# The first loads of a 2:4-pruned matmul: one weight load, two loads of x moved, four fillers fewer

## The chip, the core and the metric

The kernel runs on one core of a Trainium2 chip. The core has five engines that matter here: TensorE (PE in the profile; its weight loads are PEld), VectorE (DVE), ScalarE (ACT), GpSimd (POOL) and SyncE (SP). SyncE and ScalarE issue DMAs, each on a queue of its own. The metric is the device time of one execution in microseconds (us); the time before is the median of three runs.

## What is computed

```python
B, S, D = 16, 512, 1024              # x: [16, 512, 1024], w: [1024, 1024], b: [1024], all bf16
G = D // 4
wg = w.reshape(G, 4, D)
mag = jnp.abs(wg)
order = jnp.argsort(mag, 1)
thr = jnp.take_along_axis(mag, order[:, 2:3, :], 1)   # second largest of each four
wp = (wg * (mag >= thr)).reshape(D, D)                # 2:4 pruning along the rows
return jnp.einsum("bsd,df->bsf", x, wp) + b
```

In each column of w, of every four neighbouring rows those stay whose magnitude reaches the second largest of the four; the rest become zero. Then x times the pruned w, plus a bias.

## The kernel before, in words

The 8192 rows of x are 64 tiles of 128 rows. The weights are held as two halves of the rows (g = 0 and 1), each as four interleaved row classes (m = 0 to 3), so that the four members of a pruning group lie in one partition. The first half is pruned in four pieces of 256 columns (pieces 0 to 3), the second half in two of 512 (pieces 4 and 5).

Before pruned weights exist, TensorE cannot do useful work. So the kernel starts in this way:

- **Loads** (lines 118 to 129). `load_w` (L100) loads a piece of the weights, some of its row classes only if it is told so; `load_x` (L103) loads the first 512 columns of some tiles of x. Both go through `issue` (L96), so every DMA of theirs is recorded at L98. SyncE loads classes 0 and 1 of piece 0, then tiles 3-4, tile 2, piece 1, tiles 0-1, and further weights. ScalarE loads classes 2 and 3 of piece 0, then tiles 5-6, and after that runs a dummy activation on one element (L121), which brings in ScalarE's function table.
- **Fillers** (L136, called at L404 and L405). TensorE multiplies constants into a PSUM bank that nobody reads: six matmuls of 512 columns and then 14 short ones of 128 columns. They stand in TensorE's queue ahead of all real work.
- **An order written out by hand** (`order`, L266). For each engine a list of tokens. T3a is the transpose of tile 3 on TensorE (four instructions at L193), C3a the copy of its result by ScalarE (L198), M3.0yp a group of matmuls of tile 3 with piece 0 (L229; the letters name row classes and column halves), and abs0a, hi0a, lo0, ..., mult0yp, ... are VectorE's steps of the pruning of piece 0 (L169 for abs, L159 for the rest). TensorE's list begins T3a T4a T5a T6a T2a M3.0yp M4.0yp. VectorE's list begins abs0a abs0b, where abs0a reads classes 0 and 1 of piece 0 and abs0b classes 2 and 3. The token mult2t is the step of piece 2 whose product M3.2t reads.
- **Matmuls with whole rows** (`nat`, L240). The pruned weights are written back in row order by DMAs (`spread`, L144), and tiles 7 to 63 are multiplied with x transposed by DMA. `close` (L451) ends the tiles that were begun early; the loop at L472 does the batches of 4 and 8 tiles. VectorE adds the bias (L437 or L439), ScalarE issues the stores; for the last LATE tiles (L46) each half of the columns is stored by itself (L492).

Every DMA raises one of eight semaphores, which are used in rotation; before a semaphore is used again, the issuing queue waits for the earlier DMA on it.

## Time and profile before

| | |
|---|---|
| median of 3 runs | 232.76 us (232.62 to 232.9) |
| the profiled execution, its own time | 232.89 us |
| span in the profile, first to last instruction | 231.1 us |
| TensorE busy | 226.6 us of the span |
| VectorE busy | 107.9 us |
| ScalarE busy | 14.0 us |

In the rows of the timeline the first number is the start in us from the span's start, the second the time from the first start to the last end in the row, xN the number of instructions merged into it, and in brackets stands the idle time of the engine ahead of it and what ended that. PEld is the loading of the stationary operand, which precedes each matmul. In rows of a DMA view the last number is the time from issue to landing. In rows of the chain the second number is that instruction's share of the chain.

### The profile page before, as it was taken

The numbers are of one execution on the slowest core, as the hardware profiler recorded it, in microseconds if no ns is written. First come the engines' busy times: TensorE is split into PE (matmuls) and PEld (weight loads), VectorE is DVE, ScalarE is ACT, GpSimd is POOL, SyncE is SP. The second block draws the span as 40 slices with busy tenths as digits, with TensorE's granted clock in tenths as the row PEclk, the third lists the DMA queues.
The fourth block names the chain that finished last, engine by engine and source line by source line (L and its number), as shares of the span: only waits on it lengthen the run. The fifth ranks groups of instructions, "written<-read, shape, count | busy, mean of one in ns | idle before, by whom it ended". The sixth has DMA issues, their size and how long they took to land.

```text
span 231.1 us, 2851 instructions
## 1 busy us (share of the span) xinstructions
PE 226.6 (98%) x1142; PEld 110.9 (48%) x1162; DVE 107.9 (47%) x200; ACT 14.0 (6%) x27; POOL 17.6 (8%) x15
## 2 busy tenths in 40 slices
PE   8999999999999999999999999999999999999995
PEld 5986444444444444444444444444444444444443
DVE  3999877844424424424424424423423423433434
ACT  2874100000000000000000000000000000000000
POOL 1000199700000000000000000000000000000000
PEclk9999999999999999999999999999999999999999
DMA  6999999997399422991259821693128932122122
GB/s 203 276 197 280 164 217 223 297 320 252 124 206 232 155 91 72 237 281 64 75 116 252 222 94 71 162 298 134 65 91 198 273 122 83 54 91 91 53 86 91
DMA packets 79308, 38.19 MB, mean 165 GB/s; under 512 B 64192, under 2 KB 71744, under 8 KB 79296
## 3 DMA queue, kind: packets, MB, share of 16 engines
q1 hardware_dynamic: 68384, 20.75, 43.6%
q10 hardware_dynamic: 10912, 17.27, 20.9%
q8 instruction: 9, 0.15, 0.3%
q14 instruction: 3, 0.02, 0.0%
HBM read 3.28 MB, written 16.78 MB: 87 GB/s over the span
## 4 chain that ended last, share of the span: by engine, by line
PE 98%; issue 0%; DVE 0%
PE ps L242 88%; PE ps L229 5%; PE tp L242 2%; PE ps L138 2%; PE tp L193 1%; PE ps L193 0%; DVE o L437 0%
## 5 line engine op out<-in xcount | busy, mean ns | idle before, releaser
L242 PE MATMUL ps<-wp_nat,xb 128*128 128x512 bf16 (+1 forms) x831 | 178.9, 375 | 0.9
L242 PEld LDWEIGHTS <-xb 128*128 128x128 bf16 x848 | 82.2, 98 | 97.7
L437 DVE TENSOR_TENSOR o<-ps,bias_sb 128x512 bf16<-128x512 f32 (+1 forms) x112 | 71.6, 677 | 113.7 <-PE ps L242 111.4
L433 POOL TENSOR_TENSOR st<-st,bias_sb 128x1024 f32<-128x1024 f32 x8 | 16.7, 2142 | 0.0
L242 PE MATMUL ps<-wp_nat,xlead 128*128 128x512 bf16 x63 | 14.7, 379 | 0.1
L242 PEld LDWEIGHTS <-xlead 128*128 128x128 bf16 x88 | 8.6, 98 | 10.2
L229 PE MATMUL ps<-wp,xt 128*128 128x256 bf16 (+1 forms) x130 | 12.8, 258 | 0.0
L439 DVE TENSOR_TENSOR o<-ps,st 128x512 bf16<-128x512 f32 x16 | 11.1, 691 | 2.8 <-PE ps L242 2.2
L229 PEld LDWEIGHTS <-xt 128*128 128x128 bf16 x130 | 10.9, 98 | 1.1
L242 PE MATMUL ps<-wp_nat,xlow 128*128 128x512 bf16 x47 | 10.6, 379 | 0.1
L264 ACT COPY st<-ps 128x512 f32<-128x512 f32 x14 | 7.4, 600 | 3.2 <-PE ps L229 3.1
L242 PEld LDWEIGHTS <-xlow 128*128 128x128 bf16 x48 | 4.7, 98 | 5.7
L159 DVE TENSOR_TENSOR mag<-mag,hi 128x256 bf16<-128x256 bf16 (+2 forms) x15 | 6.1, 435 | 0.1
L159 DVE TENSOR_TENSOR wp<-w_sb,mag 128x256 bf16<-128x256 bf16 (+2 forms) x15 | 6.1, 435 | 0.1
L242 PE MATMUL tp<-wp_nat,xlead 128*128 128x512 bf16 x23 | 5.8, 380 | 0.0
L138 PE MATMUL ps<-const-bfloat16-1.0 128*128 128x128 bf16 (+1 forms) x20 | 4.2, 408 | 0.8 <-PEq L510 0.8
L169 DVE TENSOR_SCALAR mag<-w_sb 128x512 uint16<-128x512 uint16 (+2 forms) x5 | 2.3, 473 | 3.5 <-DMA w_sb<-in_w_dram 3.5
L138 PEld LDWEIGHTS <-const-bfloat16-1.0 128*128 128x128 bf16 x20 | 2.3, 146 | 2.4 <-issue 2.4
L159 DVE TENSOR_TENSOR hi<-mag 128x512 bf16<-128x512 bf16 (+2 forms) x7 | 3.2, 458 | 0.1
L159 DVE TENSOR_TENSOR lo<-mag 128x512 bf16<-128x512 bf16 (+1 forms) x6 | 3.1, 509 | 0.0
L193 PEld LDWEIGHTS <-x 128*128 128x128 bf16 x28 | 2.3, 124 | 0.3 <-DMA x<-in_x_dram 0.2
L422 POOL COPY pruned<-wp 128x1 bf16<-128x1 bf16 x1 | 0.2, 187 | 26.7 <-DVE wp L159 26.7
(18 smaller groups left out, 18.8 us busy)
## 6 DMA issues: line engine op xcount, KB each, us to landing
out_dram<-o ACTq DMA_DIRECT2D x58, 256.0 KB, 2.4
wp_nat<-wp SPq DMA_DIRECT2D x14, 128.0 KB, 3.2
out_dram<-o ACTq DMA_DIRECT2D x10, 128.0 KB, 1.7
w_sb<-in_w_dram SPq DMA_DIRECT2D x2, 512.0 KB, 5.5
w_sb<-in_w_dram SPq DMA_DIRECT2D x3, 256.0 KB, 5.1
x<-in_x_dram SPq DMA_DIRECT2D x2, 256.0 KB, 4.3
x<-in_x_dram ACTq DMA_DIRECT2D x1, 256.0 KB, 4.0
bias_sb<-in_b_dram SPq DMA_DIRECT2D x1, 256.0 KB, 4.7
```

The source lines that it names most:

```text
L138: pe(nc.tensor.matmul(warm_ps[:, :rep * P], lhsT=nc.const_aps.tensor(1.0, [P, P], bf16), rhs=nc.const_aps.tensor(1.0, [P, rep * P], bf16), ...
L159: dve(nc.vector.tensor_tensor(out, a, b_, op=op))
L169: dve(nc.vector.tensor_single_scalar(mag.bitcast(u16), w_.bitcast(u16), 0x7FFF, op=Alu.bitwise_and))
L193: pe(nc.tensor.transpose(tp[:, m, :], xg[:, m, :], ident[:]))
L229: pe(nc.tensor.matmul(ps[:, c0 + d:c1 + d], lhsT=xpk[t][:, m, :], rhs=wp[:, g, m, c0:c1], start=(new and m == ms.start), stop=(left[key] = ...
L242: pe(nc.tensor.matmul(ps, lhsT=xt[:, kt - koff, :], rhs=wp_nat[:, kt, c0:c1], start=(kt == first), stop=(kt == last)))
L264: act(nc.scalar.copy(staged[(q, h)][:, at, :, :].rearrange("p t c -> p (t c)"), ps_open.pop(key)[:]))
L422: pool(nc.gpsimd.tensor_copy(out=pruned[:], in_=wp[:, 1, 3, Dout - 1:]))
L433: pool(nc.gpsimd.tensor_tensor(st[:], st[:], bias.to_broadcast([P, 2, 2, CW]), op=Alu.add))
L437: dve(nc.vector.tensor_tensor(o[:, c0:c1], ps, bias_sb[:, c0:c1], op=Alu.add))
L439: dve(nc.vector.tensor_tensor(o[:, c0:c1].rearrange("p (n c) -> p n c", n=2), ps.rearrange("p (n c) -> p n c", n=2), add, op=Alu.add))
```

## The change

The first 256 columns of the weights are loaded by one DMA on SyncE's queue instead of by two on two queues. The load of tiles 3-4 follows directly behind it. ScalarE's load of tiles 5-6 now stands behind the dummy activation in ScalarE's program. There are ten short fillers instead of 14. LATE goes from 6 to 7, so one more tile is stored in two halves. VectorE's abs0a and abs0b stay two instructions; both now read what the one load brings.

```diff
-    LATE = 6
+    LATE = 7
...
-    load_w(0, 0, 256, 0, 2)
-    load_w(0, 0, 256, 2, 4, "act")
+    load_w(0, 0, 256)
+    load_x(3, 5)
+    act(nc.scalar.activation(spark[:], nc.const_aps.tensor(1.0, [P, 1], bf16), Act.Abs))
     load_x(5, 7, "act")
-    act(nc.scalar.activation(spark[:], nc.const_aps.tensor(1.0, [P, 1], bf16), Act.Abs))
-    load_x(3, 5)
     load_x(2, 3)
...
     filler(6, 4)
-    filler(14)
+    filler(10)
```

## The prediction

> **What bounds the kernel now.** I read the page first (busy shares, then the chain that ended last), then the chain in order of time, then the waits of the first 40 us. The page:

> ```profile
> span 231.1 us, 2851 instructions
> ...
> PE 226.6 (98%) x1142; PEld 110.9 (48%) x1162; DVE 107.9 (47%) x200; ACT 14.0 (6%) x27; POOL 17.6 (8%) x15
> ...
> PE 98%; issue 0%; DVE 0%
> ```

> TensorE (PE) is the chain from beginning to end. The change neither adds nor removes a matmul of the result, so it can act in one way only: by moving the moment at which TensorE goes from fillers to real work, or by making TensorE stop later. The chain's head and one later piece:

> ```profile
> 0.77 4.21 PE ps L138 x20
> 4.99 1.02 PE tp L193 x8
> 6.01 0.51 PE ps L193 x8
> 6.52 0.22 PE tp L193 x4
> ...
> 42.17 10.74 PE ps L242 x49
> ```

> Twenty fillers (L138), then 20 transposes (L193) of tiles 3, 4, 5, 6, 2, then matmuls. The waits of the first 40 us, two of them:

> ```profile
> DVE mag L169 <- DMA w_sb<-in_w_dram: 3.5, 1, 3.5
> ...
> PEld L193 <- DMA x<-in_x_dram: 0.2, 1, 0.2
> ```

> So two loads set the start: VectorE's pruning waits 3.5 us for the first weights, TensorE 0.24 us for tiles 3-4. After that TensorE never waits. The weight loads and matmuls at the switch:

> ```profile
> 3.29 1.43 PEld L138 LDWEIGHTS <-const-bfloat16-1.0 128*128 128x128 bf16 x13 [0.28 <-issue]
> 4.96 1.04 PE L193 MATMUL tp<-ident,x 128*128 128x128 bf16 x8
> 5.80 0.72 PE L193 MATMUL ps<-ident,x 128*128 128x128 bf16 x8
> 6.35 0.39 PE L193 MATMUL tp<-ident,x 128*128 128x128 bf16 x4
> ```

> Here the reader sees the **clock**: eight transposes from 4.96 to 5.80 are 0.105 us each; the last four in the chain take 0.22, so 0.055 each; the eight between need 0.55, which is two slow and six fast. TensorE thus runs at half speed up to 5.80 + 0.21 = 6.01 us and at full speed from there.

> **The change part by part.**

> *Ten short fillers.* A short filler is (1.43 - 0.15) / 12 = 0.107 us. The weight loads of the fillers end at 4.72; with four fewer they end at 4.72 - 0.43 = 4.29. Worth nothing by itself: TensorE already waits behind them. It decides only if tiles 3-4 land before 4.72; otherwise the pause grows.

> *LATE 7.* One 256 KB store of the seventh tile from the end becomes two of half the size. By the chain's 10.74 us for 49 matmuls, a matmul is 0.22 us, and 6 tiles of 16 matmuls are 21 us: the stores lie that far from the end. Cost 0. There is one load less and one store more, so the eight DMA semaphores are in the same rotation at the end.

> *The loads.* The issues of before, and their times to landing (DMA view at each issue's window):

> ```profile
> 0.73 0.45 SPq L98 DMA_DIRECT2D w_sb<-in_w_dram  x1
> 1.24 0.96 SPq L98 DMA_DIRECT2D x<-in_x_dram  x2
> 2.25 0.68 SPq L98 DMA_DIRECT2D w_sb<-in_w_dram  x1
> 0.74 0.50 ACTq L98 DMA_DIRECT2D w_sb<-in_w_dram  x1
> 1.26 0.49 ACTq L98 DMA_DIRECT2D x<-in_x_dram  x1
> 1.79 1.28 ACT L121 ACT_TABLE_LOAD   x1 [1.79 <-issue]
> 3.08 0.20 ACT L121 ACTIVATE spark<-const-bfloat16-1.0 128x1 bf16<-128x1 bf16 x1
> ```

> ```profile
> w_sb<-in_w_dram ACTq DMA_DIRECT2D x1, 128.0 KB, 2.9
> x<-in_x_dram SPq DMA_DIRECT2D x1, 256.0 KB, 3.7
> x<-in_x_dram ACTq DMA_DIRECT2D x1, 256.0 KB, 4.0
> w_sb<-in_w_dram SPq DMA_DIRECT2D x1, 256.0 KB, 4.5
> x<-in_x_dram SPq DMA_DIRECT2D x1, 256.0 KB, 5.0
> ```

> Before: the second half of the weights lands at 0.74 + 2.9 = 3.64, tiles 3-4 at 1.24 + 3.7 = 4.94, tiles 5-6 at 1.26 + 4.0 = 5.26. And the DMA engines, from 2.6 to 4.3 us:

> ```profile
> 2.60:4.30 1.70, 1.70 (x13) 1.17 (x11) 0.80 (x4) 0.68 (x2) 0.00 (x0) 1.00 1.00 334
> ```

> The last two columns are the share of the DMA engines and GB/s: they are full, at 334. (The column before them, the clock, says 1.00 there, which the spacing of the matmuls contradicts; I go by the spacing.) So what counts is the order in which bytes are asked for. The three loads together (768 KB) are done at 5.26 in whatever order they go, and a load moved behind another frees its 256 KB / 334 GB/s = 0.78 us.

> *When does ScalarE issue tiles 5-6?* This decides the case. No row of before shows a DMA issued behind a running activation. The bounds are 0.8 us (ScalarE's sequencer hands over the table load and the Abs, neither of which waits for anything, and goes on) and 0.74 + 1.28 + 0.20 = 2.2 us (it stays until both are done). The nearest rows:

> ```profile
> 20.36 0.59 ACT L264 COPY st<-tp 128x512 f32<-128x512 f32 x1
> L98 ACTq EVENT_SEMAPHORE  x71: 17/17/17, 20.4 to 228.4; - x71
> 28.14 16.74 POOL L433 TENSOR_TENSOR st<-st,bias_sb 128x1024 f32<-128x1024 f32 x8
> L521 POOLq DRAIN  x3: 34/78/16641, 28.3 to 230.8; - x3
> ```

> ScalarE's first semaphore instruction runs at 20.4, while the copy begun at 20.36 still has 0.5 us to go. GpSimd's sequencer stands at its closing drain at 28.3, with eight adds of 16.74 us in total handed over. Sequencers run ahead of their engines here, so I take **0.8 us**: tiles 5-6 are then asked for 0.46 us earlier than before, not later.

> [...]

> *Weights.* One 256 KB load on one queue. Bounds for its landing: 3.5 us (where the first half lands now: VectorE starts at 3.50) and 0.73 + 4.5 = 5.2 (the next 256 KB of weights, which stand behind other loads). Nearest are the two halves, at 3.64; tiles 5-6, asked for earlier, take part of the engines, at most 0.78 us of it, and by how early they come about a third. I take 3.9, so VectorE starts s = 0.4 us later. Its first operation waited for half of the weights and now waits for all; behind it stands VectorE's whole pruning chain, and behind that the matmuls of L229.

> *What stands behind on SP's queue.* The first issue grows from 0.45 to at most 0.68 us (the row at 2.25, as many bytes), so tile 2, the next weights and tiles 0-1 are issued up to 0.23 later. With the engines full they land by bytes, and those ahead of them are the same; cost 0, unless tile 0 slips (its room is below).

> *Tiles 3-4.* Last of the three in this order, so between 4.94 and 5.26; I take 5.15, and TensorE starts at 5.19. Slow transposes until 6.01: 0.82 / 0.105 = 7.8. The other 12.2 at 0.055 take 0.67, to 6.68. The same sum for before: 1.05 / 0.105 = 10, 10 x 0.055 = 0.55, to 6.56. Loss **0.12 us**. The 0.23 us of later start is halved since it falls in the slow clock.

> *Does VectorE's 0.4 us come through?* These pairs are a product of VectorE (start, duration) and the weight load of TensorE's first matmul that reads it (the first and the 75th load of L229, by the order list M3.0yp and M3.2t); the last is the first transpose of tile 0, loaded at 2.96 + 5.0 = 7.96:

> ```profile
> 5.80 0.28 DVE L159 TENSOR_TENSOR wp<-w_sb,mag 128x256 bf16<-128x256 bf16 x1
> 6.52 0.15 PEld L229 LDWEIGHTS <-xt 128*128 128x128 bf16 x2
> 12.49 0.28 DVE L159 TENSOR_TENSOR wp<-w_sb,mag 128x256 bf16<-128x256 bf16 x1
> 13.07 0.10 PEld L229 LDWEIGHTS <-xt 128*128 128x128 bf16 x1
> 8.23 0.11 PEld L193 LDWEIGHTS <-x 128*128 128x128 bf16 x1
> ```

> Room is 0.44, 0.30 and 0.27 us. With VectorE 0.4 later and TensorE 0.12 later, M3.2t's room is 0.30 - 0.40 + 0.12 = 0.02: just enough. So the sum is +0.12. The profiled execution took 232.89 us, 231.1 of it span and 1.8 around it; it would become 233.01. The median of the runs is 232.76, 0.13 below it, so the forecast is 232.76 + 0.12 = **232.9 us**.

> **The rivals.**

> *B, the change does what it says:* ScalarE holds the issue to 2.2 us. Tiles 3-4 then stand behind the weights alone and land 0.78 earlier than 5.26, at 4.5; TensorE starts at 4.54. Tiles 5-6 now stand behind tile 2 as well (128 KB, 0.38 us) and land between 5.26 and 5.64, say 5.45; eight slow transposes end at 5.38, so TensorE waits until 5.49. Then 5 slow and 7 fast transposes, to 6.40: 0.16 earlier. Weights have the engines to themselves (3.65, s = 0.15), which fits M3.2t's room. 232.6. More than about 0.3 can't be won in any case: the rooms 0.27 and 0.30 are then used up, and VectorE or tile 0 is the bound. For it: the program order. Against: the rows on the sequencers.

> *C, the clock is released later (slower):* TensorE's pause between fillers and tiles 3-4 grows from 0.24 to 5.19 - 4.29 = 0.9 us, since the fillers were cut for an arrival that doesn't come. If the release needs unbroken work, it decides from a pause somewhere above the 0.24 that before survives. The full clock came 6.01 - 0.77 = 5.24 us after the first filler; counted anew from 5.19 it comes at 10.43, and 4.4 us at half speed cost 2.2: 235.0. For it: nothing here shows what a longer pause does. Against: a pause of 0.9 in 5 us still leaves over 80% busy.

> [...]

> *D, the weights bound VectorE (slower):* one queue brings the 256 KB later than two. The price is s - 0.30, where it exceeds 0.12; above 0.2% (0.47 us) from s = 0.77, a landing after 4.27. At the upper end of its bounds, 5.2, it would be 1.4 us. For it: the next 256 KB took 4.5 us. Against: those stood behind three loads. Its middle is s = 0.7 to 0.9: 233.2 to 233.4.

> **How the numbers follow.** 0.2% (0.47 us) is about what a measurement of this kernel can tell from no change. Forecast A (232.9, itself 232.6 to 233.2) 0.46, B 0.24, C 0.14, D 0.16. Faster by over 0.2% needs B with the weights also earlier than now: 0.05 of B. Slower by over 0.2%: C, 0.11 of D, and 0.03 of A: 0.28. Same: 0.67. The range runs from 232.4 (B at its best) to 233.7 (D with s near 1.2); it leaves out C and a little of B and D, 0.2 in all.

> **What would show it.** In the profile of the changed kernel: ScalarE's DMA row at about 0.8 us ahead of the table load's end (A) or at 2.2 (B); TensorE's wait for x at about 0.9 us (A) or 0.25 (B); the first transpose at 5.19; VectorE's first row at 3.9; the matmul spacing halving near 6.0 (C if at 9 to 10); any wait of PEld for VectorE near 13 us (D). I am wrong if TensorE's chain shows a pause after 7 us, or if the ends of before and after differ by more than their first matmuls of L229 do.

## The result, and the profile after

| | before | after |
|---|---|---|
| median | 232.69 us (4 runs, 232.4 to 232.9) | 234.38 us (4 runs: 233.58, 234.35, 234.42, 234.78) |
| ratio, 95% interval | 1 | 1.0073 [1.0058, 1.0088] |
| profiled execution, own time | 232.89 us | 233.58 us |
| its span | 231.1 us | 231.8 us |

The changed kernel is 0.7% slower, outside the range given. The profiled execution is the fastest of the four, so it can't hold the whole loss: it shows 0.69 us, and the others took 0.8 to 1.2 us more. Both parts need an explanation.

The page of after, its span, busy times and chain:

```profile
span 231.8 us, 2864 instructions
...
PE 226.8 (98%) x1158; PEld 110.0 (47%) x1158; DVE 107.8 (47%) x200; ACT 13.9 (6%) x27; POOL 17.6 (8%) x15
...
PE 96%; DMA 2%; DVE 1%; issue 0%
```

TensorE is as busy as before, but the chain now begins with a DMA and VectorE (3% together), where it was TensorE's from beginning to end. The chain in order of time, first of before (only the pieces not shown yet), then of after; the first number of each row is its start:

```profile
6.74 1.76 PE ps L229 x20
...
9.16 10.30 PE ps L229 x108
```

```profile
0.73 3.88 DMA w_sb<-in_w_dram
...
4.63 0.50 DVE mag L168 x2
...
7.01 0.21 DVE wp L158
...
7.27 1.92 PE ps L228 x20
...
9.85 10.32 PE ps L228 x108
```

(Lines of after have numbers one lower: L228 is before's L229.) The block of 108 matmuls starts at 9.85 instead of 9.16 and lasts as long: 0.69 us, which is the whole difference of the two profiled executions, 233.58 - 232.89. Everything is decided before 10 us. (That execution of before had itself lost time to half-speed transposes up to 6.01 us. Not every execution does; see e3.) The timeline of the two issuing queues of after:

```profile
0.73 1.28 ACT L120 ACT_TABLE_LOAD   x1 [0.73 <-PEq L509]
0.80 0.45 ACTq L98 DMA_DIRECT2D x<-in_x_dram  x1
...
0.73 0.69 SPq L98 DMA_DIRECT2D w_sb<-in_w_dram  x1
1.48 1.10 SPq L98 DMA_DIRECT2D x<-in_x_dram  x2
```

ScalarE's sequencer issues tiles 5-6 at 0.80 us, with the table load still running until 2.01: the load that stands behind the activation in the program overtakes it. The issue ends at 0.80 + 0.45 = 1.25, that of the weights at 0.73 + 0.69 = 1.42. The DMA view of after, at the windows of these issues (last column: issue to landing):

```profile
x<-in_x_dram ACTq DMA_DIRECT2D x1, 256.0 KB, 2.8
...
w_sb<-in_w_dram SPq DMA_DIRECT2D x1, 256.0 KB, 3.9
x<-in_x_dram SPq DMA_DIRECT2D x1, 256.0 KB, 3.9
```

Tiles 5-6 land at 3.6, the weights at 4.6, tiles 3-4 at 5.4. And the DMA queues of after from 1.9 to 2.75 us, then from 2.8 to 3.7 us (packets, MB, share of the 16 engines; q1 is SyncE's queue, q10 ScalarE's):

```profile
q10 hardware_dynamic: 201, 0.21, 93.4%
...
q1 hardware_dynamic: 416, 0.21, 80.6%
q10 hardware_dynamic: 52, 0.04, 13.5%
```

For the first 0.85 us ScalarE's queue alone moves bytes. The weights hardly share the engines with tiles 5-6, they stand behind them. Here the first packet of SyncE's queue starts at 2.80, 0.88 us after that of ScalarE's at 1.92; in the traces of e1, e5, e9 and e10 it is 0.8 to 1.2 us. What that does to the waits of the first 40 us of after:

```profile
DVE mag L168 <- DMA w_sb<-in_w_dram: 4.6, 1, 4.6
...
PEld L192 <- DMA x<-in_x_dram: 1.2, 1, 1.2
...
PE ps L228 <- DVE wp L158: 0.6, 1, 0.6
```

The last row is new: TensorE waits for the pruned weights. TensorE's timeline, before and then after:

```profile
6.58 1.92 PE L229 MATMUL ps<-wp,xt 128*128 128x128 bf16 x20
```

```profile
5.41 0.64 PE L192 MATMUL tp<-ident,x 128*128 128x128 bf16 x8 [0.98 <-DMA x<-in_x_dram]
5.88 0.61 PE L192 MATMUL ps<-ident,x 128*128 128x128 bf16 x8
6.33 0.39 PE L192 MATMUL tp<-ident,x 128*128 128x128 bf16 x4
7.27 1.92 PE L228 MATMUL ps<-wp,xt 128*128 128x128 bf16 x20 [0.55 <-DVE wp L158]
```

Here the transposes run at full speed from their first (eight in 0.64 us; before, the first eight took 1.04), although TensorE had stood still for 0.98 us. They end 0.55 us before there is anything to multiply. In this execution the clock is no loss at all; only the weights are late.

### The profile page after: what moved, and what is told of

Read it like the earlier page. It is cut to its first block, busy times and chain, and to the rows that moved or that the text cites. A ratio compares the mean times of both kernels' runs of the same rounds, so it can differ in the third digit from the quotient of the medians.

```text
span 231.8 us, 2864 instructions
## 1 busy us (share of the span) xinstructions
PE 226.8 (98%) x1158; PEld 110.0 (47%) x1158; DVE 107.8 (47%) x200; ACT 13.9 (6%) x27; POOL 17.6 (8%) x15
## 4 chain that ended last, share of the span: by engine, by line
PE 96%; DMA 2%; DVE 1%; issue 0%
PE ps L241 88%; PE ps L228 5%; PE tp L241 2%; DMA w_sb<-in_w_dram 2%; DVE hi L158 0%; DVE lo L158 0%; DVE mag L168 0%; DVE mag L158 0%; DVE o L436 0%; PE ps L192 0%; PE tp L192 0%; DVE wp L158 0%
## 5 line engine op out<-in xcount | busy, mean ns | idle before, releaser
L241 PE MATMUL ps<-wp_nat,xb 128*128 128x512 bf16 (+2 forms) x848 | 179.8, 375 | 0.0
L228 PE MATMUL ps<-wp,xt 128*128 128x256 bf16 (+1 forms) x130 | 12.8, 258 | 0.6 <-DVE wp L158 0.6
L228 PEld LDWEIGHTS <-xt 128*128 128x128 bf16 x130 | 10.8, 98 | 2.0 <-issue 0.7
L137 PE MATMUL ps<-const-bfloat16-1.0 128*128 128x128 bf16 (+1 forms) x16 | 3.6, 415 | 0.8 <-PEq L509 0.8
L192 PE MATMUL tp<-ident,x 128*128 128x128 bf16 x16 | 1.4, 221 | 1.0 <-DMA x<-in_x_dram 1.0
## 6 DMA issues: line engine op xcount, KB each, us to landing
out_dram<-o ACTq DMA_DIRECT2D x57, 256.0 KB, 2.4
wp_nat<-wp SPq DMA_DIRECT2D x14, 128.0 KB, 2.9
out_dram<-o ACTq DMA_DIRECT2D x12, 128.0 KB, 1.7
w_sb<-in_w_dram SPq DMA_DIRECT2D x4, 256.0 KB, 4.5
x<-in_x_dram SPq DMA_DIRECT2D x2, 256.0 KB, 4.1
x<-in_x_dram ACTq DMA_DIRECT2D x1, 256.0 KB, 2.8
bias_sb<-in_b_dram SPq DMA_DIRECT2D x1, 256.0 KB, 4.2
```

Source lines behind the costliest of these rows:

```text
L137: pe(nc.tensor.matmul(warm_ps[:, :rep * P], lhsT=nc.const_aps.tensor(1.0, [P, P], bf16), rhs=nc.const_aps.tensor(1.0, [P, rep * P], bf16), ...
L192: pe(nc.tensor.transpose(tp[:, m, :], xg[:, m, :], ident[:]))
L228: pe(nc.tensor.matmul(ps[:, c0 + d:c1 + d], lhsT=xpk[t][:, m, :], rhs=wp[:, g, m, c0:c1], start=(new and m == ms.start), stop=(left[key] = ...
L241: pe(nc.tensor.matmul(ps, lhsT=xt[:, kt - koff, :], rhs=wp_nat[:, kt, c0:c1], start=(kt == first), stop=(kt == last)))
```

## The experiments

Two theories. **Theory 1, the order of the loads:** tiles 5-6 are served ahead of the weights, and VectorE's lateness is the loss. **Theory 2, the clock:** the executions above 234 us are those in which TensorE's longer pause keeps the clock at half speed longer. (Between weight loads, the prediction's measure, the pause was 0.24 us in before and is 1.16 in after; between matmuls, the measure used from here on, it was nothing and is 0.98.) The rival to both was that LATE, the fillers or the use of one queue cost something by themselves. Below, "ratio" is always to the kernel before, whose runs beside the experiments had medians of 232.51 to 232.6.

**e1, after with the pause filled.**

```diff
-    filler(10)
+    filler(20)
```

> The changed kernel with 20 short fillers instead of ten, so that TensorE works until tiles 3-4 land (near 5.4 us). Theory 1 (order): ScalarE's load of tiles 5-6 goes out ahead of the first weights, these land at 4.6 and VectorE is 1.1 us late; that costs the 0.7 us of the profiled execution in every execution. Theory 2 (clock), on top of it: the pause of 1.1 us between fillers and transposes keeps the full clock away longer in most executions, which is the other 0.8 to 1.2 us. Both together expect 233.3 to 233.6 here, with a small spread, and the clock released by about 7.5 us. If the clock has no part in it, the time stays at 234.4. Transposes start at 5.4 in either case.

Measured: 233.50 us (four runs, 233.42 to 233.61), ratio 1.0039 [1.0024, 1.0054]. TensorE's timeline:

```profile
5.36 0.61 PE L192 MATMUL tp<-ident,x 128*128 128x128 bf16 x8
...
7.22 1.92 PE L228 MATMUL ps<-wp,xt 128*128 128x128 bf16 x20 [0.50 <-DVE wp L158]
```

The pause ahead of the transposes is gone and with it, in these four executions, every time above 233.61; the wait for VectorE stays. So the loads cost 233.50 - 232.55 = 0.95 us between medians, without the pause, and the rest hangs on the pause.

**e2, after, with ScalarE's load really held back:** the dummy activation writes into the tile that the load fills, so the load must wait for it.

```diff
-    def load_x(ta, tb, eng="sp"):
+    def load_x(ta, tb, eng="sp", hold=False):
...
+        if hold:
+            act(nc.scalar.activation(xs[:, 0, :1], nc.const_aps.tensor(1.0, [P, 1], bf16), Act.Abs))
...
-    act(nc.scalar.activation(spark[:], nc.const_aps.tensor(1.0, [P, 1], bf16), Act.Abs))
-    load_x(5, 7, "act")
+    load_x(5, 7, "act", hold=True)
```

> The changed kernel with the dummy activation writing one element of the tile that tiles 5-6 are loaded to, so that the load has to wait until the activation has ended (issue near 2.2 us instead of 0.80). Theory 1 expects the weights back at 3.6 to 3.8, tiles 3-4 at 4.4 to 4.6, tiles 5-6 near 5.5, and 232.4 to 232.7 in all. The rival (one load on one queue is slow by itself) expects the weights at 4.3 or later again and 233.2 or more.

Measured: 234.81 us (234.05 to 235.12), ratio 1.0090 [1.0067, 1.0113]. A miss: it was to be the fast version, and is no faster than the change. Timeline of ScalarE's queue, and the DMA view:

```profile
2.27 0.43 ACTq L98 DMA_DIRECT2D x<-in_x_dram  x1
```

```profile
w_sb<-in_w_dram SPq DMA_DIRECT2D x1, 256.0 KB, 3.1
x<-in_x_dram SPq DMA_DIRECT2D x1, 256.0 KB, 3.4
...
x<-in_x_dram ACTq DMA_DIRECT2D x1, 256.0 KB, 4.3
```

```profile
4.89 1.04 PE L193 MATMUL tp<-ident,x 128*128 128x128 bf16 x8 [0.33 <-DMA x<-in_x_dram]
6.67 1.01 PE L193 MATMUL ps<-ident,x 128*128 128x128 bf16 x8 [0.74 <-DMA x<-in_x_dram]
```

The weights do come first, at 3.85. In before VectorE started at 3.50, on the first half alone (the second came at 3.64, in time for its second operation); against that, one load on one queue cost some 0.35 to 0.4 us here (landed at 3.85, VectorE from 3.88). The bytes begin to move later: the first packet of any load starts at 2.23 here and at 1.83 in before, where the first issue ended at 1.18 and not at 1.42. That is the share that isn't due to tiles 5-6; being behind them cost the other 4.61 - 3.85 = 0.76 us, the time of 256 KB at the prediction's 334 GB/s (0.78). But tiles 3-4 land at 4.85, hardly earlier than the 4.94 of before, and tiles 5-6 at 2.27 + 4.3 = 6.57, both later than expected: TensorE waits a second time, and the clock is still slow. So the order that the change seems to write down gains nothing over the order that it got (234.81 against 234.38, with ranges that overlap).

**e3, before with fewer fillers alone.**

```diff
-    filler(14)
+    filler(10)
```

> The kernel before with ten short fillers instead of 14 and nothing else. All landings stay as before; TensorE's pause ahead of tiles 3-4 grows from 0.24 to 0.67 us. Theory 2 expects some executions in which the clock is released later than 7.6 us and a median 0.2 to 1.2 us above the kernel before. If the pause is harmless, the time is that of the kernel before, 232.7, within 0.15.

Measured: 232.38 us (ten runs, 232.28 to 233.07), ratio 0.9992 [0.9981, 1.0004]: no difference. TensorE's timeline of e3, then of e6 (below):

```profile
4.79 0.83 PE L193 MATMUL tp<-ident,x 128*128 128x128 bf16 x8 [0.23 <-DMA x<-in_x_dram]
```

```profile
4.79 0.64 PE L193 MATMUL tp<-ident,x 128*128 128x128 bf16 x8 [0.40 <-DMA x<-in_x_dram]
```

The pauses of 0.23 and 0.40 us did no harm (medians 232.38 in e3 and 232.67 in e6, beside before's 232.55 and 232.60), so theory 2 in the form "any longer pause loses the clock" is wrong. In e3's traced execution (232.42) the first products start at 6.13, where before's (232.89) had 6.58: its tiles 3-4 came 0.17 us earlier and its clock at 5.26. Against an execution like that the loads cost more than the 0.69 above: 233.58 - 232.42 = 1.16 us.

**e6, before with LATE 7 and ten fillers.**

```diff
-    LATE = 6
+    LATE = 7
...
-    filler(14)
+    filler(10)
```

> The kernel before with ten short fillers and LATE 7, its loads as they were: all of the change but the loads. Theory 1 puts the whole loss on the order of the loads, so this is the kernel before within 0.15 us (232.3 to 232.7). If LATE 7 costs something at the end, it shows as more than 0.2 above the kernel before with ten fillers (232.38).

Measured: 232.67 us (232.36 to 233.13), ratio 1.0006 [0.9993, 1.0018]. LATE and the fillers cost nothing as long as the loads are those of before, so this part of the rival falls: the whole loss comes in with the loads. (The share of the one queue is in e2.)

**e4, after with the weights in two halves, both on SyncE's queue.**

```diff
-    load_w(0, 0, 256)
+    load_w(0, 0, 256, 0, 2)
+    load_w(0, 0, 256, 2, 4)
```

> The changed kernel with the first weights in two loads of 128 KB, both on SyncE's queue; tiles 5-6 still go out beside the table load. If loads are served in the order in which their issue ends (that of tiles 5-6 ended at 1.24, that of the whole weights at 1.42), the first half, whose issue would end near 1.18, is served first and lands at 3.4 to 3.6; tiles 5-6 at about 4.0, the second half at 4.2 to 4.4. VectorE then starts at 3.5 but waits for the second half; TensorE's first product is 0.1 to 0.5 us earlier than in the changed kernel. If it is the queue that matters and not the end of issue, both halves land at 4.2 to 4.6.

Measured: 233.78 us, in two groups: 233.58, 233.67, 233.67, 233.78 and 234.66, 235.18, 235.51; ratio 1.0074 [1.0047, 1.0100]. Its timeline (issue, and VectorE's first two operations):

```profile
0.73 0.96 SPq L98 DMA_DIRECT2D w_sb<-in_w_dram  x2
...
0.80 0.46 ACTq L98 DMA_DIRECT2D x<-in_x_dram  x1
...
3.79 0.29 DVE L169 TENSOR_SCALAR mag<-w_sb 128x512 uint16<-128x512 uint16 x1 [3.79 <-DMA w_sb<-in_w_dram]
4.81 0.29 DVE L169 TENSOR_SCALAR mag<-w_sb 128x512 uint16<-128x512 uint16 x1 [0.73 <-DMA w_sb<-in_w_dram]
```

The first half is issued by about 1.2 us (half of the row's 0.96), just ahead of tiles 5-6 at 1.26; the second half at 1.69. They land in that order: first half 3.76, tiles 5-6 at 0.80 + 3.6 = 4.4, second half 4.79. So what counted across the two queues is when an issue ended, not which queue it was on. Nothing is won, since VectorE's pruning needs the second half too: the first product starts at 7.24, where after had 7.27 and 0.1 to 0.5 less was expected. The landings were some 0.2 to 0.6 us later than expected.

**e5 and e9, the change again.** e5 is the unchanged file, timed once more; e9 runs it for the trace of an execution above 234 us.

> The changed kernel once more, unchanged, for more executions and another trace. Theory 2, as the first traces sharpen it: the clock is judged at marks 3.41 us apart whose place differs from execution to execution, and is released at the first mark behind which TensorE was busy for roughly 70% or more of the 3.41 us (seen so far: 68% kept it slow, 77% released it). With fillers from 0.77 to 4.36 and transposes from 5.4, marks between 3.2 and 5.3 release it, those between 5.3 and 6.6 fail and the next comes at 8.7 to 10.0. So two groups: 233.5 to 233.7 with a release before 5.4, and 234.2 to 234.9 with one after 8.6. A single group with a late release in all, or times between the groups, would speak against it.

> The changed kernel unchanged, one more trace, to see an execution of the slow group. Its two traces so far were of the fast group (release at 4.1 and 5.0 us, 233.6 us). About an even chance of either group; in the slow one theory 2 expects the same landings and the same first product near 7.3 to 7.6 us, matmuls at half speed until a release between 8.7 and 10.0, and 234.2 to 234.9 us. A slow execution with an early release, or with landings later than 4.7 and 5.4, would refute it.

Measured: e5 233.54, 233.58, 233.63 and 234.42, 234.61, 234.86; e9 234.46. With the first four that makes 11 executions of the changed kernel: four at 233.54 to 233.63, seven at 234.35 to 234.86, none between. e9's trace belongs to the upper group. Its TensorE and then its chain:

```profile
5.32 1.04 PE L192 MATMUL tp<-ident,x 128*128 128x128 bf16 x8 [0.76 <-DMA x<-in_x_dram]
6.16 1.06 PE L192 MATMUL ps<-ident,x 128*128 128x128 bf16 x8
...
7.44 2.22 PE L228 MATMUL ps<-wp,xt 128*128 128x128 bf16 x16
```

```profile
7.65 2.46 PE ps L228 x20
...
10.77 10.30 PE ps L228 x108
```

Tiles 3-4 land as they did, but all transposes run at half speed, and so does the first block of products up to the release at 8.97 (2.46 us, where after had 1.92). The block of 108 starts at 10.77, where after had it at 9.85: 0.92 us, and the times differ by 234.46 - 233.58 = 0.88. The transposes' own slowness (1.04 + 0.85 + 0.43 = 2.32 us in the chain) costs less than it looks, as it takes the place of the wait for VectorE. Of the seven in the upper group this is the only one traced.

**e8, before with a pause nearly as long as that of the change.**

```diff
-    filler(14)
+    filler(4)
```

> The kernel before with four short fillers instead of 14: nothing but the pause of TensorE changes, from 0.24 us to 1.3 (fillers until 3.67, transposes from 4.9). Theory 2: marks between 3.2 and 4.6 us release the clock, those between 4.6 and 6.6 fail (busy 62%) and the next comes at 8.0 to 10.0; so two groups, 232.3 to 232.6 and 233.4 to 234.4, the second somewhat more frequent. If the pause is harmless, all lie near 232.5.

Measured: 232.46 and 234.01, 234.05, 234.34, 234.45; ratio 1.0066 [1.0042, 1.0090]. The traced execution is the one at 232.46:

```profile
4.73 0.64 PE L193 MATMUL tp<-ident,x 128*128 128x128 bf16 x8 [0.81 <-DMA x<-in_x_dram]
```

With the loads of before, fewer fillers and so a longer pause alone make two groups, one undisturbed and one 1.6 to 2 us later (a little more than expected; none of these was traced). By these times theory 2 holds in a second form: not any pause (0.23 and 0.40 us in e3 and e6), but a long one (0.81 here), and not in every execution.

**e10, after with a still longer pause.**

```diff
-    filler(10)
+    filler(4)
```

> The changed kernel with four short fillers instead of ten: the pause grows from 1.05 to 1.7 us, nothing else. Theory 2: marks between 3.2 and 4.6 us release the clock, all later ones up to 6.6 fail, so the slow group (234.2 to 234.9) holds more than half of the executions, and the fast group stays at 233.5 to 233.7, since VectorE sets the first product there. If it is the number of fillers or the length of the pause as such that costs, both groups move up.

Measured: 234.24, 234.66, 234.75, 235.31; ratio 1.0085 [1.0068, 1.0102]. The lower group that was expected is missing in these four. The one trace, that of 235.31, shows one way to lose it. Its windows from 4.22 us, where the trace's clock record (the moments at which the granted clock changed) has the release (columns: window, length, busy time and count of each engine, granted clock, DMA share, GB/s):

```profile
4.22:7.64 3.42, 1.58 (x25) 1.47 (x26) 2.91 (x16) 1.48 (x5) 0.00 (x0) 1.00 1.11 319
7.64:11.05 3.41, 3.41 (x23) 2.67 (x21) 3.38 (x17) 0.59 (x1) 0.00 (x0) 0.50 1.30 260
```

The clock was released at 4.22, taken back at 7.64, and came again at 11.05. So in this execution a clock that had come was lost again, after 3.42 us.

```profile
2.90:6.32 3.42, 2.70 (x20) 1.89 (x18) 2.44 (x13) 0.72 (x2) 0.00 (x0) 1.00 1.03 314
```

```profile
2.14:5.55 3.41, 2.65 (x17) 1.55 (x16) 0.98 (x5) 0.09 (x1) 0.00 (x0) 1.00 0.97 301
```

```profile
1.75:5.16 3.41, 2.81 (x15) 1.44 (x12) 0.64 (x3) 0.47 (x2) 0.00 (x0) 1.00 0.87 274
```

```profile
1.57:4.98 3.41, 2.99 (x15) 1.59 (x13) 0.40 (x2) 0.66 (x2) 0.00 (x0) 1.00 0.85 271
```

(The clock column says 1.00 in all four, wrongly: the first record of a change comes later than the window.) Taken so, 2.65 us in e9 and 2.70 in e2 weren't enough; 2.81 in e4 and 2.99 in e5 were. By this measure, whose ends of matmuls are modelled, that is 78 and 79% of a stretch against 82 and 88%. (By the spacing of the starts, the measure behind the 70% in the expectation of e5, it is 67 and 72% that weren't enough, 76 and 82% that were.) A pause of 0.40 us (e6) leaves 88% of a stretch wherever the marks lie; one of 0.76 (e9) leaves 78% if it falls whole into a stretch, so it depends on the mark; e1's transposes follow the fillers without one. The groups of e1, e3, e5 and e8 fit that; those above 234 in e8 were not traced.

For the loss of a clock that has come, there is one trace: in e10 the full clock went after a stretch with 1.58 of 3.42 us busy. In after it stayed through the stretch from 4.14, with 1.87 of 3.41:

```profile
4.14:7.55 3.41, 1.87 (x30) 1.58 (x29) 2.92 (x16) 1.48 (x5) 0.00 (x0) 1.00 1.04 316
```

**e7, an order that the rows suggested:** before, with tiles 5-6 on SyncE's queue behind tiles 3-4.

```diff
-    load_x(5, 7, "act")
+    load_x(5, 7)
...
-    filler(14)
+    filler(10)
```

> The kernel before with ten short fillers and the load of tiles 5-6 on SyncE's queue, directly behind that of tiles 3-4; the weights stay in two loads on two queues. If loads are served in the order in which their issue ends, the weights land at 3.3 to 3.6 as before, tiles 3-4 at 4.4 to 4.6 (before 4.75 to 4.9), tiles 5-6 at 5.0 to 5.3, just in time. VectorE's room allows little of it: 232.1 to 232.5. If one queue is slower than two, tiles 5-6 land after 5.5 and the time is 232.7 or more.

Measured: 233.0 us (ten runs, 232.23 to 233.43), ratio 1.0013 [1.0000, 1.0025]: not the gain expected. Its traced execution is the fastest of the ten, 232.23, and does what was meant:

```profile
4.56 0.69 PE tp L193 x8
...
6.06 1.77 PE ps L229 x20
```

The first products start at 6.06, where before had 6.74 (and e3, with the loads of before, 6.29). Why the other nine took 0.45 to 1.2 us more wasn't traced and stays open; before itself spread from 232.24 to 233.18 in its 21 runs beside them. No version here was measurably faster than the kernel before.

## Why the prediction was wrong, point by point

- **When ScalarE issues.** Right: 0.80 us, beside a table load that ends at 2.01, from the rows that show sequencers ahead of their engines.
- **The weights, the first of two steps that failed.** "Tiles 5-6, asked for earlier, take part of the engines, at most 0.78 us of it, and by how early they come about a third. I take 3.9." They took all of it. The price of the 256 KB was right (0.76 measured against 0.78), the share was not: their issue ended at 1.25, that of the weights, made longer by being one load, at 1.42, and the earlier was served nearly whole before the other began. 3.65 with the engines to themselves was low as well (3.85). Both together give 4.61 instead of 3.9, so s was 1.13 (VectorE from 3.50 to 4.63) instead of 0.4. This step alone would have left the time near e1's 233.50, inside the range of 232.4 to 233.7; what took the median to 234.38 is the second step, the clock.
- **Rival D was the mechanism of the first part, and its price was near.** s - 0.30 gives 0.83 us with the measured s; 0.69 came in the profiled executions' comparison, 0.95 between the medians of e1 and before. But the wait was not near 13 us, where D looked for it: it came at the first product, at 7.27. That pair's room was 0.44, and s - 0.44 = 0.69 is what the two executions show. Its point of decision, a landing after 4.27, had been passed. It got 0.16 because of the step above.
- **Tiles 3-4.** "Between 4.94 and 5.26; I take 5.15": 5.36. The first packet of the three loads starts at 1.92 here and at 1.83 in before, which is about the 0.10 beyond the bound. That they come last was right; the order ahead of them was mistaken: tiles 5-6, then the weights.
- **The clock at 6.01, the second step that failed.** "TensorE thus runs at half speed up to 6.01" is true of one execution; the sum then carried 6.01 over as a fixed moment, for before and after. It lies between 4.14 and 9.73 in these traces. The 9 to 10 us at which the prediction would look for rival C, and the 7.5 and 7.6 in the expectations of e1 and e3, follow from no row of theirs; the late releases measured are 8.97 (e9) and 9.73 (e2), e3's is 5.26, and e1 has no clock record. The forecast's +0.12 for slow transposes therefore held for no execution but one whose clock comes at 6.01, and the range left out that the clock can come late.
- **Rival C was half right.** The longer pause (0.9 forecast between weight loads, 1.16 and 1.0 measured in after and e9) does go with a late clock, traced in e9 and, by their times, in seven of 11 executions; not because a count starts anew (that would be 10.43, and e9 has 8.97), but, by the estimate above, because a stretch was too idle (2.65 of 3.41 us in e9). The cost was put at 2.2 us; on top of D it was 0.8 to 1.3, as TensorE would otherwise have waited for VectorE (alone, by the times of e8, it was 1.6 to 2.0). C and D were weighed as alternatives, with 0.30 between them; both happened at once, in most executions, which no case had. "A pause of 0.9 in 5 us still leaves over 80% busy" divided by the time from the first filler to the release in before (5.24); of e10's 3.41 us between two changes it leaves 74%, less than the 78% that weren't enough in e9.
- **Rival B** didn't happen, and its own price was wrong: held back in truth (e2), the loads give 234.8, not 232.6, a late clock included. B put tiles 3-4 at 4.5 and tiles 5-6 at 5.45; they land at 4.85 and 6.57, as the issue at 2.27 took 4.3 us to land.
- **Fillers and LATE: 0.** Right by themselves (e6). With tiles 3-4 landing at 5.36, the ten fillers open the pause that e1's 20 close.

So the loss is about 1 us by the loads (0.95 between medians) in every execution seen, and 0.8 to 1.3 more in seven of 11, by the clock in the one of them that was traced (e9).

## What to carry to other kernels

At the start of a kernel, write down for each load when its issue ends, over all queues: here the loads were served in that order, and the load that stood behind an activation in the program wasn't held by it (issued at 0.80, with the table load running until 2.01). Let fillers reach to the real landing of the data: here they were cut for an arrival that came late (5.36), which left a pause of 0.76 to 0.98 us, and by their times full speed came late in seven of 11 executions, not in all. One trace shows one such execution, so a time that comes in two groups needs a trace of each before it is explained.

## What the runs showed of the hardware that was not expected

- Of two loads on two queues, the one whose issue ended 0.17 us earlier had the DMA engines almost to itself (93.4% its own bytes from 1.9 to 2.75 us, none of the other's). e4's landings (3.76, 4.4, 4.79) fit the order of its ends of issue (about 1.2, 1.26, 1.69); why the end of the issue decides was not tested further.
- The first 256 KB load of weights takes 0.69 us to issue, and either half 0.45 to 0.50: two queues saved issue time, and here the end of the issue set the order and the moment at which bytes began to move.
- In e10 the clock's three changes lie 3.42 and 3.41 us apart; in the other traces the first lies anywhere from 4.14 to 9.73 us, and the two lengths of the full clock (225.28 and 228.69) differ by 3.41. In stretches of that length 2.81 us of TensorE work (e4) were followed by full speed and 2.70 (e2) were not; after 1.58 us it was lost again (e10), through 1.87 it was kept (after), one execution each.
